# One more wait on GpSimd: the first operation of each attention round starts behind VectorE's FK product

## The chip, the cores and the metric

One NeuronCore of a Trainium2 chip runs the whole program in one launch. The metric is the device time of that core in microseconds, from the launch to the end of the program. A profiled execution has also a span, from its first to its last instruction, which is some two microseconds shorter than its device time.

## The reference

The inputs are float32. Three stages follow each other; only the first is touched by the change.

```python
# stage 1: linear attention with a decaying state, B=4, H=8, S=768, D=48
for t in range(S):
    cur = einsum('bhd,bhe->bhde', u * k[t], v[t])
    y[t] = einsum('bhd,bhde->bhe', r[t], state + cur)
    state = w * state + einsum('bhd,bhe->bhde', k[t], v[t])
# stage 2: x = y as [3072, 384]; tokens with x @ w_skip > 0 go to the expert
#          (of 8) with the largest gate logit: x + gate * (relu(x @ w1[e]) @ w2[e])
# stage 3: ((x @ w1) * (x @ w2)) @ w3 @ w_out
```

## The kernel before

**Stage 1** is worked in 24 tiles of 128 rows. A tile n is a chunk c = n // 2 of 64 time steps of one pair of batches bp = n % 2, all 8 heads side by side. The decay inside a chunk is put into two tables made once (UT, and KU for the key side), so that a tile needs these steps:

- `prep(n)`, VectorE, L360: FK = TB * UT, 128x1024, both operands in SBUF. TB holds r and k of the tile, transposed, and comes by DMA.
- `scores(n)`, TensorE, L367: 16 small matrix products of the two halves of FK into the PSUM bank sc, of which there is one.
- `evac(n)`, VectorE, L372: Fs = sc * mask, one operand in PSUM. It frees sc.
- `prep_k(n)`, GpSimd, L379: kd = k * KU, 128x384, both operands in SBUF; needed by `ds_mm(n)`, which adds the tile to the state on TensorE (L436). The last two tiles need no kd.
- `prep_m(n)`, GpSimd, L385 and L386: m = r * u, then m = k * m, 128x384 each, in SBUF.
- `bonus(n)`, VectorE, L390: z = sum of m over the head's 48 elements.
- `state_copy(n)`: in every second chunk VectorE rescales the state in PSUM (S, L408), and ScalarE copies it to SBUF.
- `y_mm(n)`, TensorE, L420 and L423; `prep_v(n)`, ScalarE, L400; `x_out(n)`, VectorE, L441: xg = y + zv, and two stores of xg from the queue of SyncE.

Beside them every round has fillers. `w_step` prepares the weights of stage 3 on VectorE (their 64-bit words are cut to float32 by the three operations of L112, L115 and L119, the first with one tensor operand and the other two with two operands in SBUF). `keep` puts products of these weights, or empty ones, between the others on TensorE (L712, L256), a fixed number for each round. The routing of earlier tiles (`route_a` to `route_d`, `place`; L471 to L567) is made of small VectorE operations that come in some rounds alone.

The order on each engine is that in which the program writes the calls, since scheduling is manual. The loop over rounds n = 0 to 21 writes, in this order: the load of TB for tile n + 4, `prep(n + 2)`, `state_copy(n + 1)`, `scores(n + 1)`, `prep_k(n + 1)`, `prep_m(n + 2)`, `evac(n + 1)`, `bonus(n + 1)` (in round 21 also `bonus(23)`), in rounds 0 to 2 some constants on GpSimd, one `w_step`, `y_mm(n)`, fillers, routing, the second `w_step` where there is one, `x_out(n)`, `ds_mm(n)`, the load of KV for tile n + 4, `place`, the third `w_step`, routing. A round is named by its n, so round n has FK of tile n + 2, kd of tile n + 1 and m of tile n + 2. FK has three buffers, kd and m have two each.

A GpSimd operation of this loop waits for its data (KV by DMA) and for its buffer (kd for `ds_mm` two tiles back, m for `bonus` two tiles back), and for nothing else. So GpSimd may be ahead of VectorE's place in the round or behind it.

Of the kernel before, what the change touches and what calls it, by code (L numbers as in the profile page):

```python
# [13 lines left out]
ALU = mybir.AluOpType  # L14
# [10 lines left out]
NT = NTOK // P  # L25
# [32 lines left out]
def fused_kernel(ctx, tc, att, kv, wt, u, wg, we, w3, wo, w12, r, k, v, wu, out):  # L58
    nc = tc.nc
# [134 lines left out]
    def load_expert(e, q):  # L194
        raw = stg[(4 * e + q) % 3 // 2].tile([P, 2, 2 * D], F32, name="raw")
        nc.sync.dma_start(out=raw, in_=we[e, :, 2 * q:2 * q + 2, :])
        return raw
# [29 lines left out]
    with tc.manual_schedule():  # L227
# [5 lines left out]
        KV = [[ac.tile([P, 3, NH, HD], F32, name=f"KV{bp}_{j}") for j in range(2)] for bp in range(2)]  # L233
        Ss = [ac.tile([P, NH, HD], F32, name=f"Ss{bp}") for bp in range(2)]
        TB = [ac.tile([P, 2, NH, CH], F32, name=f"TB{j}") for j in range(3)]
        un = ac.tile([P, NH, HD], F32, name="un")

        def load_t(n):
            nc.sync.dma_start(out=TB[n % 3].rearrange("p a h t -> p (a h t)"), in_=att[n])
# [30 lines left out]
        for q in range(2):  # L270
            m = mask[64 * q:64 * q + 64]
# [12 lines left out]
        UT = ac.tile([P, 2, 2, NH, CH], F32, name="UT")  # L284
# [6 lines left out]
        for i in range(6):  # L291
            wn = pw[:, i - 1] if i else wc
            n = 1 << i
# [13 lines left out]
        KU = ac.tile([P, 2, NH, HD], F32, name="KU")  # L307
# [48 lines left out]
        def prep(n):  # L356

            t = TB[n % 3]
            FK = FK_[n] = wk.tile([P, 2, NH, CH], F32, name="FK", bufs=3)
            nc.vector.tensor_tensor(out=FK, in0=t, in1=UT[:, n // 2 % 2], op=ALU.mult)  # L360

        def scores(n):
            FK = FK_[n]
            sc = ps_1.tile([P, 512], F32, tag="sc", name="sc").rearrange("p (h t) -> p h t", h=NH)
            for h in range(NH):
                for m, d in zip(half, dims):
                    nc.tensor.matmul(sc[m, h], FK[d, 1, h], FK[d, 0, h], start=True, stop=True)  # L367
            return sc

        def evac(n, sc):  # L370
            Fs = Fs_[n] = wk.tile([P, NH, CH], F32, name="Fs")
            nc.vector.tensor_tensor(out=Fs, in0=sc, in1=mask[:, None, :].to_broadcast([P, NH, CH]), op=ALU.mult)  # L372

        def prep_k(n):

            c, bp = divmod(n, 2)
            if c < NC - 1:
                kd = kd_[n] = wk.tile([P, NH, HD], F32, name="kd")
                nc.gpsimd.tensor_tensor(out=kd, in0=KV[bp][c % 2][:, 1], in1=KU[:, c % 2], op=ALU.mult)  # L379

        def prep_m(n):

            c, bp = divmod(n, 2)
            m = P_[n] = wk.tile([P, NH, HD], F32, name="m")
            nc.gpsimd.tensor_tensor(out=m, in0=KV[bp][c % 2][:, 0], in1=un, op=ALU.mult)  # L385
            nc.gpsimd.tensor_tensor(out=m, in0=KV[bp][c % 2][:, 1], in1=m, op=ALU.mult)  # L386

        def bonus(n):
            z = z_[n] = wk.tile([P, 32], F32, name="z")[:, 0:NH]
            nc.vector.tensor_reduce(out=z, in_=P_.pop(n), axis=AX.X, op=ALU.add)  # L390

        def prep_v(n, eng=None):
            c, bp = divmod(n, 2)
            v, z = KV[bp][c % 2][:, 2], z_.pop(n)
            zv = zv_[n] = wk.tile([P, NH, HD], F32, name="zv")
            if eng:
                eng.tensor_tensor(out=zv, in0=v, in1=z[:, :, None].to_broadcast([P, NH, HD]), op=ALU.mult)
            else:
                for h in range(NH):
                    nc.scalar.activation(out=zv[:, h], in_=v[:, h], func=AF.Copy, scale=z[:, h:h + 1])  # L400

        def state_copy(n):
            c, bp = divmod(n, 2)
            s = S[bp]
            if c == 0:
                return
            if c % 2 == 0:
                nc.vector.tensor_tensor(out=s, in0=s, in1=w128[:, :, None].to_broadcast([P, NH, HD]),  # L408
                                        op=ALU.mult)
            nc.scalar.copy(out=Ss[bp], in_=s)  # L410

        def y_mm(n, tag="y"):

            c, bp = divmod(n, 2)
            v, Fs, FK = KV[bp][c % 2][:, 2], Fs_.pop(n), FK_.pop(n)
            y = G if n % 2 and n < NT - 2 else ps_1.tile([P, 512], F32, tag=tag, name="y")
            yv = y[:, 0:D].rearrange("p (h d) -> p h d", h=NH)
            for h in range(NH):
                for m in half:
                    nc.tensor.matmul(yv[m, h], Fs[m, h], v[m, h], start=(h == 0), stop=True, skip_group_check=True)  # L420
            for h in range(NH if c else 0):
                for m, d in zip(half, dims):
                    nc.tensor.matmul(yv[m, h], FK[d, 0, h], Ss[bp][d, h], start=False, stop=True,  # L423
                                     skip_group_check=True)
            y_[n] = y
            if n < NT - 2:
                yb[0] = y
# [10 lines left out]
        def x_out(n):  # L438
            c, bp = divmod(n, 2)
            xg = x_[n] = wk.tile([P, D], F32, name="xg", bufs=2)  # L440
            nc.vector.tensor_tensor(out=xg, in0=y_.pop(n)[:, 0:D], in1=zv_.pop(n).rearrange("p h d -> p (h d)"),  # L441
                                    op=ALU.add)
            for q in range(2):
                r0 = (2 * bp + q) * NS + c * CH
                nc.sync.dma_start(out=xm[r0:r0 + CH, :], in_=xg[64 * q:64 * q + 64, :])

        def x_trans(n, bank=None):
            xg = x_.pop(n)
            xb_[n] = T if bank is None else bank
            pT = xb_[n][:, 0:D].rearrange("p (k t) -> p k t", k=ND)  # L450
            for k in range(ND):
                nc.tensor.transpose(pT[:, k], xg[:, P * k:P * k + P], ident)
            xT_[n] = wk.tile([P, ND, P], F32, name="xT", bufs=2)
            nc.scalar.copy(out=xT_[n], in_=pT)
# [219 lines left out]
        def w_step(k):  # L674
            for _ in range(k):
                next(wprep, None)
# [3 lines left out]
        def w_evac(k):  # L680

            while k < len(w_out):
                f, ps = w_out[k]
                nc.scalar.copy(out=W_hi[:, f], in_=ps)
                w_out[k:k + 1] = []
                w_lo.append((f, ps))
# [8 lines left out]
        def w_ready():  # L695
            done.update(fresh[0])
            fresh[:] = fresh[1:] + [[]]
# [29 lines left out]
        def keep(k):  # L727

            due[0] += k
            while due[0] > 0:  # L730
                if next(wmm, None):
                    due[0] -= 4
                else:
                    idle_mm()
                    due[0] -= 2


        prep(0)
        table_k(0)
        load_t(3)  # L740
# [23 lines left out]
        def run_todo(late=False):  # L764
            now, todo[:] = sorted(todo, key=lambda x: x[0] is not logits), []
            for fn, args in now:
                if late and fn is route_b:
                    todo.append((fn, args))
                    continue
                fn(*args)  # L770
                if fn is logits_out:
                    if args[0] in last_of:
                        todo.append((route_a, (last_of[args[0]],)))
                elif fn in NEXT:
                    todo.append((NEXT[fn], args))

        for n in range(NT - 2):
            w_ready()
            if n == NT - 3:
                raws = {q: load_expert(0, q) for q in range(2)}  # L780
            if n + 4 < NT:
                load_t(n + 4)
            prep(n + 2)
            state_copy(n + 1)
            sc = scores(n + 1)
            prep_k(n + 1)
            prep_m(n + 2)
            evac(n + 1, sc)
            bonus(n + 1)
            if n == NT - 3:  # L790
                bonus(NT - 1)
            next(more_consts, None)
            w_step(WN[n][0])
            w_ready()
            y_mm(n)
            keep(4 * WK[n][0])
            run_todo()
            if n > 0:
                x_trans(n - 1)
            prep_v(n + 1)  # L800
            keep(4 * WK[n][1])
            w_step(WN[n][1])
            w_evac(0)
            x_out(n)
            ds_mm(n)
            place_mm(n % 2)
            if n + 4 < NT:
                load_v(n + 4)
            if n < NT - 3:
                place(3)  # L810
            w_step(WN[n][2])
            run_todo(n < NT - 3)
            if n > 0:
                todo.append((logits, (n - 1,)))
            w_evac2()
# [100 lines left out]
    with tc.manual_schedule():  # L916
# [126 lines left out]
        first = {}  # L1043
# [324 lines left out]
```

## Time and profile before

| | us |
|---|---|
| median of 3 runs | 648.27 |
| lowest and highest of them | 647.77, 656.43 |
| the profiled execution, device time | 645.56 |
| its span | 643.8 |
| TensorE busy in the span | 620.2 (96%) |
| VectorE busy | 366.2 (57%) |
| GpSimd busy | 142.8 (22%) |

The loop of stage 1 fills some 14 to 160 us of the span; what follows is the routing's end, the experts to some 330 us and stage 3. Start times in the rows are us from the start of the span. An instruction's duration in the trace runs on while it waits for access inside the engine, so the same operation can show two durations; the idle time in brackets ahead of an operation is what the engine spent with nothing to run, and the name behind the arrow is what ended it.

### The profile page before, as it was taken

The numbers are of one execution on the slowest core, as the hardware profiler recorded it, in microseconds if no ns is written. First come the engines' busy times: TensorE is split into PE (matmuls) and PEld (weight loads), VectorE is DVE, ScalarE is ACT, GpSimd is POOL, SyncE is SP. The second block draws the span as 40 slices with busy tenths as digits, with TensorE's granted clock in tenths as the row PEclk, the third lists the DMA queues.
The fourth block names the chain that finished last, engine by engine and source line by source line (L and its number), as shares of the span: only waits on it lengthen the run. The fifth ranks groups of instructions, "written<-read, shape, count | busy, mean of one in ns | idle before, by whom it ended". The sixth has DMA issues, their size and how long they took to land.

```text
span 643.8 us, 14006 instructions
## 1 busy us (share of the span) xinstructions
PE 620.2 (96%) x5866; PEld 535.6 (83%) x5866; DVE 366.2 (57%) x641; ACT 254.2 (39%) x592; POOL 142.8 (22%) x134
## 2 busy tenths in 40 slices
PE   7989999899989999999999999999999999999996
PEld 6878877788769999999988888888888888888884
DVE  6699999999478789998863312322321321330320
ACT  2555644444346666666542322222322221331220
POOL 4885555554040322333220000000000000000000
PEclk9899999999989999999999999999999999999999
DMA  8889978557158877778211002002002002000001
GB/s 306 347 276 350 342 248 320 175 168 233 48 171 270 294 246 277 273 256 308 92 62 56 0 34 66 1 34 65 1 17 81 2 16 82 0 17 34 0 2 53
DMA packets 26791, 90.53 MB, mean 141 GB/s; under 512 B 4009, under 2 KB 10298, under 8 KB 25696
## 3 DMA queue, kind: packets, MB, share of 16 engines
q1 hardware_dynamic: 24672, 84.11, 37.6%
q0 software_dynamic: 2048, 5.44, 2.5%
q8 instruction: 48, 0.79, 0.5%
q14 instruction: 23, 0.19, 0.1%
HBM read 77.81 MB, written 12.58 MB: 140 GB/s over the span
## 4 chain that ended last, share of the span: by engine, by line
PE 75%; DVE 13%; issue 5%; DMA 4%; POOL 1%; ACT 1%; SPq 1%; DVEq 0%; ACTq 0%; POOLq 0%
PE ab L1131 31%; PE po L1151 15%; PE hp L931 9%; PE y L950 9%; PE wp L712 3%; DMA TB<-in_att 3%; DVE FK L360 3%; PE sc L367 1%; DVE Fs L372 1%; DMA KV<-in_kv 1%; DVE w L119 1%; PE pT L1111 1%; DVE z L390 1%; DVE w L112 1%; DVE w L115 1%
## 5 line engine op out<-in xcount | busy, mean ns | idle before, releaser
L1138 DVE TENSOR_TENSOR p_sb<-ab,a_sb 128x512 f32<-128x512 f32 x48 | 33.2, 691 | 155.6 <-PE ab L1131 155.6
L1131 PE MATMUL ab<-bxh,w12h 128*128 128x512 f32 x288 | 112.3, 390 | 0.6 <-ACT bxh L1170 0.6
L1131 PE MATMUL ab<-bxh,w12l 128*128 128x512 f32 x288 | 112.0, 389 | 0.0
L1131 PE MATMUL ab<-bxl,w12h 128*128 128x512 f32 x288 | 112.0, 389 | 0.0
L1139 ACT CAST ph<-p_sb 128x512 fp32r<-128x512 f32 x48 | 29.8, 621 | 105.9 <-DVE p_sb L1138 105.9
L86 DVE TENSOR_TENSOR elo<-raw,ehi 128x768 fp32r<-128x768 f32 x64 | 60.8, 954 | 8.7 <-ACT ehi L85 8.4
L1131 PEld LDWEIGHTS ab<-bxh,w12h 128*128 128x128 f32 x288 | 54.0, 188 | 12.7 <-ACT bxh L1170 1.5
L1131 PEld LDWEIGHTS ab<-bxl,w12h 128*128 128x128 f32 x288 | 54.1, 188 | 11.6 <-DVE bxl L1172 0.4
L1131 PEld LDWEIGHTS ab<-bxh,w12l 128*128 128x128 f32 x288 | 54.1, 188 | 11.1
L1151 PE MATMUL po<-ph,W_hi 128*128 128x512 f32 x144 | 57.0, 396 | 0.0
L1151 PE MATMUL po<-pl,W_hi 128*128 128x512 f32 x144 | 56.1, 390 | 0.0
L1151 PE MATMUL po<-ph,W_lo 128*128 128x512 f32 x144 | 56.0, 389 | 0.0
L931 PE MATMUL hp<-xh,ehi 128*128 128x256 f32 x192 | 54.5, 286 | 1.3 <-ACT xh L881 1.1
L931 PE MATMUL hp<-xl,ehi 128*128 128x256 f32 x192 | 54.1, 284 | 0.0
L931 PE MATMUL hp<-xh,elo 128*128 128x256 f32 x192 | 54.0, 283 | 0.0
L85 ACT CAST ehi<-raw 128x768 fp32r<-128x768 f32 x64 | 52.6, 828 | 2.8 <-DMA raw<-in_we 2.8
L1140 DVE TENSOR_TENSOR pl<-p_sb,ph 128x512 fp32r<-128x512 f32 x48 | 33.2, 692 | 32.9 <-ACT ph L1139 32.9
L400 ACT ACTIVATE zv<-KV,z 128x48 f32<-128x48 f32 x184 | 44.0, 324 | 16.8 <-DVE z L390 14.9
L712 PE MATMUL wp<-wo_s,w 128*128 128x384 f32 x128 | 50.4, 505 | 0.0
L934 ACT ACTIVATE hh<-hp 128x256 fp32r<-128x256 f32 x64 | 24.6, 385 | 49.5 <-PE hp L931 49.3
L950 PE MATMUL y<-ehi,hh 128*128 128x384 f32 x128 | 43.5, 339 | 0.0
L950 PE MATMUL y<-ehi,hl 128*128 128x384 f32 x128 | 43.2, 337 | 0.0
(207 smaller groups left out, 1174.8 us busy)
## 6 DMA issues: line engine op xcount, KB each, us to landing
raw<-in_we SPq DMA_DIRECT2D x32, 768.0 KB, 4.8
KV<-in_kv SPq DMA_DIRECT2D x24, 576.0 KB, 5.5
TB<-in_att SPq DMA_DIRECT2D x24, 512.0 KB, 7.3
raww<-in_w SPq DMA_DIRECT2D x8, 1024.0 KB, 7.8
raw<-in_w SPq DMA_DIRECT2D x8, 768.0 KB, 6.7
xm<-xg SPq DMA_DIRECT2D x48, 96.0 KB, 3.2
out<-ob SPq DMA_DIRECT2D x18, 256.0 KB, 2.0
x<-xm SPq DMA_DIRECT2D x20, 192.0 KB, 3.0
```

The source lines that it names most:

```text
L85: nc.scalar.copy(out=hi, in_=raw)
L86: (eng or nc.vector).tensor_tensor(out=lo, in0=raw, in1=hi.bitcast(F32), op=ALU.subtract)
L400: nc.scalar.activation(out=zv[:, h], in_=v[:, h], func=AF.Copy, scale=z[:, h:h + 1])
L712: nc.tensor.matmul(ps, w3[:, g], wo_s[:, g], start=(g == 0), stop=(g == NF - 1))
L931: nc.tensor.matmul(hp, a, b, start=(i == 0), stop=(i == 8))
L934: nc.scalar.activation(out=hh, in_=hp, func=AF.Relu)
L950: nc.tensor.matmul(ys[e, t], a[:, P * t:P * t + P], b[:, D:2 * D], start=(f == 0 and i == 0), stop=(f == NF - 1 and i == 2))
L1131: nc.tensor.matmul(q, a, b, start=(i == 0), stop=(i == 8))
L1138: nc.vector.tensor_tensor(out=p_sb, in0=ps[1], in1=a_sb, op=ALU.mult)
L1139: nc.scalar.copy(out=ph, in_=p_sb)
L1140: nc.vector.tensor_tensor(out=pl, in0=p_sb, in1=ph.bitcast(F32), op=ALU.subtract)
L1151: nc.tensor.matmul(po, a[:, f, c], b, start=(i == 0), stop=(i == 3 * NF - 1))
```

## The change

The first GpSimd operation of round n gets one more wait, for the end of FK of the same round. In rounds 0 to 20 this is kd of tile n + 1, and in round 21, which has no kd, the first half of m of tile 23. `prep`, `prep_k` and `prep_m` return their first instruction for it, and `behind` adds a semaphore dependency. No operation is added, removed or put in another place of its engine's order; the calls ahead of the loop (tiles 0 and 1) have no such wait.

```diff
             t = TB[n % 3]
             FK = FK_[n] = wk.tile([P, 2, NH, CH], F32, name="FK", bufs=3)
-            nc.vector.tensor_tensor(out=FK, in0=t, in1=UT[:, n // 2 % 2], op=ALU.mult)
+            return nc.vector.tensor_tensor(out=FK, in0=t, in1=UT[:, n // 2 % 2], op=ALU.mult)
+
+        def behind(later, earlier):
+
+            tc.add_manual_dep(later.ins, earlier.ins.name, mybir.DependencyInfo(
+                mybir.DependencyClass.Sync, mybir.DependencyReason.DATA), reason="two operands from SBUF each")
...
-                nc.gpsimd.tensor_tensor(out=kd, in0=KV[bp][c % 2][:, 1], in1=KU[:, c % 2], op=ALU.mult)
+                return nc.gpsimd.tensor_tensor(out=kd, in0=KV[bp][c % 2][:, 1], in1=KU[:, c % 2], op=ALU.mult)
...
-            nc.gpsimd.tensor_tensor(out=m, in0=KV[bp][c % 2][:, 0], in1=un, op=ALU.mult)
+            first = nc.gpsimd.tensor_tensor(out=m, in0=KV[bp][c % 2][:, 0], in1=un, op=ALU.mult)
             nc.gpsimd.tensor_tensor(out=m, in0=KV[bp][c % 2][:, 1], in1=m, op=ALU.mult)
+            return first
...
-            prep(n + 2)
+            fk = prep(n + 2)
             state_copy(n + 1)
             sc = scores(n + 1)
-            prep_k(n + 1)
-            prep_m(n + 2)
+            behind(prep_k(n + 1) or prep_m(n + 2), fk)
+            if n < NT - 3:
+                prep_m(n + 2)
             evac(n + 1, sc)
             bonus(n + 1)
```

## Rows read from the trace of the kernel before

**Rows 1.** Windows: length; busy (count) of PE, PEld, DVE, ACT, POOL; TensorE clock; DMA share.
```profile
26.00:60.00 34.00, 30.09 (x715) 26.51 (x715) 33.83 (x38) 17.46 (x58) 24.17 (x23) 1.00 0.83 294
60.00:110.00 50.00, 47.72 (x1016) 39.79 (x1016) 49.55 (x75) 26.24 (x87) 30.49 (x23) 1.00 0.87 304
110.00:158.00 48.00, 45.93 (x991) 37.99 (x992) 47.10 (x91) 22.34 (x85) 26.30 (x21) 1.00 0.59 190
```

**Rows 2.** Waits in 26 to 158 us: total, times, longest.
```profile
POOL kd L379 <- PE S L436: 30.0, 13, 3.9
...
PE sc L367 <- DVE Fs L372: 7.7, 7, 2.4
```

**Rows 3.** Timeline, VectorE and GpSimd around FK of round 4.
```profile
36.56 1.98 POOL L379 TENSOR_TENSOR kd<-KV,KU 128x384 f32<-128x384 f32 x1
...
38.07 1.55 DVE L119 SCALAR_TENSOR_TENSOR w<-raww,w 128x1024 int32<-128x1024 int32 x1
...
38.50 1.97 POOL L385 TENSOR_TENSOR m<-KV,un 128x384 f32<-128x384 f32 x1
...
39.55 2.01 DVE L360 TENSOR_TENSOR FK<-TB,UT 128x1024 f32<-128x1024 f32 x1
...
40.55 1.86 POOL L386 TENSOR_TENSOR m<-KV,m 128x384 f32<-128x384 f32 x1
...
42.37 1.00 POOL L379 TENSOR_TENSOR kd<-KV,KU 128x384 f32<-128x384 f32 x1
```

**Rows 4.** Timeline, VectorE and GpSimd at the start of round 10.
```profile
81.89 1.21 DVE L360 TENSOR_TENSOR FK<-TB,UT 128x1024 f32<-128x1024 f32 x1
...
83.02 0.67 DVE L372 TENSOR_TENSOR Fs<-sc,mask 128x512 f32<-128x512 f32 x1
83.62 0.53 DVE L390 TENSOR_REDUCE z<-m 128x8 f32<-128x384 f32 x1
...
84.08 0.67 DVE L112 TENSOR_SCALAR w<-w 128x1024 int32<-128x1024 int32 x1
84.23 1.38 POOL L385 TENSOR_TENSOR m<-KV,un 128x384 f32<-128x384 f32 x1 [0.28 <-DVE z L390]
```

**Rows 5.** VectorE's groups by line, 25.5 to 158 us: busy, mean ns, idle before.
```profile
L360 DVE TENSOR_TENSOR FK<-TB,UT 128x1024 f32<-128x1024 f32 x20 | 30.3, 1517 | 4.2 <-DMA TB<-in_att 4.2
L372 DVE TENSOR_TENSOR Fs<-sc,mask 128x512 f32<-128x512 f32 x20 | 13.5, 676 | 0.0
L119 DVE SCALAR_TENSOR_TENSOR w<-raww,w 128x1024 int32<-128x1024 int32 x8 | 11.8, 1480 | 0.0
L115 DVE SCALAR_TENSOR_TENSOR w<-raww,w 128x1024 int32<-128x1024 int32 x8 | 11.5, 1436 | 0.0
...
L112 DVE TENSOR_SCALAR w<-w 128x1024 int32<-128x1024 int32 x8 | 6.7, 833 | 0.0
...
L552 DVE TENSOR_TENSOR val<-r_sg,val 128x6 bf16<-128x6 f32 (+1 forms) x3 | 2.0, 654 | 0.1
...
L471 DVE TENSOR_TENSOR r_oh<-io_f,r_mi 128x48 f32<-128x48 f32 (+1 forms) x3 | 1.1, 373 | 0.1
```

**Rows 6.** VectorE by source line, L115: durations least/median/most, first and last start.
```profile
L115 DVE SCALAR_TENSOR_TENSOR w<-raww,w x8: 1206/1212/1968, 35.8 to 131.3; 128x1024 int32<-128x1024 int32 x8
```

**Rows 7.** Timeline, TensorE, the last places where it waits for VectorE.
```profile
98.58 1.15 PE L367 MATMUL sc<-FK 48*64 48x64 f32 x32 [0.60 <-DVE Fs L372]
...
124.97 0.92 PE L436 MATMUL S<-KV,kd 64*48 64x48 f32 x32
127.96 1.15 PE L367 MATMUL sc<-FK 48*64 48x64 f32 x32 [2.07 <-DVE Fs L372]
```

**Rows 8.** Timeline, VectorE in round 21.
```profile
156.37 1.21 DVE L360 TENSOR_TENSOR FK<-TB,UT 128x1024 f32<-128x1024 f32 x1
...
158.11 0.99 DVE L390 TENSOR_REDUCE z<-m 128x8 f32<-128x384 f32 x2
160.16 0.56 DVE L441 TENSOR_TENSOR xg<-G,zv 128x384 f32<-128x384 f32 x1 [1.06 <-PE G L465]
```

## The prediction

> **What bounds the kernel now.** I read the windows first, since the change lives in one stage alone. In each of the three stretches from 26 to 158 us [rows 1] the reader is to see two engines that are nearly full: VectorE works 33.83 of 34, 49.55 of 50 and 47.10 of 48 us, and TensorE 30.09, 47.72 and 45.93. TensorE's idle time is what is left: 3.9 + 2.3 + 2.1 = 8.3 us. The waits come next [rows 2]: nearly all of that, 7.7 us in 7 places, is TensorE's scores waiting for VectorE's Fs, which frees the PSUM bank. So VectorE's pace sets the loop, and TensorE is close behind it: **no saving on VectorE can give more than some 8.3 us**, about 1.3% of the run. The last place where TensorE waits is 127.96 us [rows 7]; from there it runs without a gap to the end of the loop. The end therefore moves with VectorE's progress up to that point. GpSimd's largest wait, 30.0 us for its kd buffer, costs nothing: it is early.
>
> Then the timeline. Around FK of round 4 [rows 3] GpSimd and VectorE take turns. The weight operation L119 runs from 38.07, m asks at 38.50 and takes 1.97 us; FK asks at 39.55, when L119 lets go, and takes 2.01; the next m asks at 40.55 and takes 1.86. Alone, FK takes 1.21 [rows 4] and a GpSimd product 1.00 [rows 3]. So a GpSimd product and a VectorE operation with two operands in SBUF don't overlap: who asks later stands still, and FK lost 2.01 - 1.21 = 0.80 us. Fs, with one operand in PSUM, is never stretched (mean 676 ns in 20, 0.67 alone) [rows 4, 5].
>
> What this costs before: for each VectorE instruction of rounds 2 to 20 I took its duration less the shortest of its form. The groups of [rows 5] hold it: FK 20 x (1.517 - 1.204) = 6.3 us; the wide weight operations 8 x (1.480 - 1.206) + 8 x (1.436 - 1.206) + 8 x (0.833 - 0.67) = 5.3 us (the clean L115 in [rows 6], L112 in [rows 4]); the rest, routing products above all (seven groups of three, means from 654 down to 373 ns, some 200 ns clean) and the narrower weight operations, about 7.8. Together **19.4 us in 19 rounds**.
>
> **The change, step by step.** It adds 22 waits and no work. Behind the waiting kd stand both m operations of its round (in rounds 0 to 2 constants too); who needs them is `ds_mm` and `bonus` of the next round. From FK's start, kd would ask at 1.29 us (FK's 1.21 and 0.08: z of [rows 4] ends at 84.15 and the m that waits for it starts at 84.23) and the last m would end by about 4.5 even with two stops. The z that reads it comes after the next round's FK and Fs, 1.74 us into that round; a round lasts 6.6 us on average (20 FKs [rows 5] in 132 us), so z comes at some 8.3 us against 4.5. Nobody waits: this part costs nothing as long as a round is longer than 4.5 - 1.74 = 2.8 us. Round 21 is the exception, since its z of tile 23 stands in the same round. m would ask at 1.29 and its second half end by some 3.4 us after FK's start, while z now starts at 1.74 + 0.46 = 2.2 [rows 8]: 1.2 us later. Behind it xg waited for TensorE for 1.06 us anyway [rows 8], so about 0.2 us is left. SyncE's loads of KV wait for a kd of the round before, which stays earlier than they are; DMA is 0.59 to 0.87 busy [rows 1].
>
> What is moved is where GpSimd's three products stand beside VectorE. Clean starts from FK's start [rows 4]: Fs 1.13, z 1.73, the first weight operation 2.19, each 0.47 later in the ten rounds with the state's rescale. I take 0.82 us as the time for which a product shuts VectorE out (FK's 0.80, rounded up by its entry), the one that asks first goes first, and go through the rounds.
> - kd runs from 1.29 to about 2.2, beside Fs and z, which it can't stop. FK is free of it: the 0.8 us of [rows 3] is gone.
> - The first m asks at about 2.27. Without rescale the weight operation asked at 2.19 and goes first; m enters as it ends. With rescale m is first, and the operation, due at 2.66, waits until about 3.1: 0.4 us.
> - The second m meets what comes then: 0.66 us where a second weight operation follows directly (rounds 2 to 6), otherwise it begins beside xg, which covers 0.47 of its 0.82, and 0.3 us falls on the operation behind.
>
> Rounds 2 to 6, three weight operations each, give 3 x 0.97 + 1.06, and 1.90 in round 3, where round 2's constants on GpSimd still push the product of before into FK: 5.9 us (6.6 now). Rounds 7, 10 to 13, 16 and 17, one operation ahead of xg, give 0.7 with rescale and 0.3 without: 3.8 us (3.4 now). The seven rounds with much routing (8, 9, 14, 15, 18 to 20) give 6.6 us (9.4 now), the least certain part, as products of 0.2 us either meet an m or don't. Sum 16.2 against 19.4: **3.2 us less on VectorE**. Up to round 15, which is what counts for the wait at 127.96, it is 13.3 against 17.1: 3.85 us earlier. TensorE could take that: its own work is done at 124.97 + 0.92 = 125.89, and with the earlier wait at 98.58 moved by 2.1 us it is free at 123.8, ahead of 127.96 - 3.85 = 124.1 [rows 7].
>
> Unknown is the hold. At 0.87 us instead of 0.82 some forty meetings, two a round, cost 0.05 each, 2 us, and 1.85 is left. I take the middle, -2.85, and round 21's +0.2: **-2.6 us** (rounded). The profiled execution, 645.56 us for a span of 643.8, would come to about 643. The median of the runs is 2.7 above that execution, and I forecast against the median: 648.27 - 2.6 = **645.7**. Ends of this term: -8.3 (all of TensorE's idle time) and +3 (below).
>
> By the Trainium skill (SBUF — State Buffer, Who interferes with whom) issue order decides which of the two blocks and the later one blocks fully; this trace agrees, FK's 2.01 us behind an m, and on that rule alone the change picks another loser and frees nobody.
>
> **The rivals.**
> - *The collisions only move.* Each FK freed is a weight or routing operation stopped. For it: of the three kinds above one gets worse, and the gain is mostly in the routing rounds. Against it: kd's 19 products get cover that they often lack now. Time: 19.4 us stay, 648.3.
> - *Slower: m wins the race to the first weight operation.* Without rescale that operation is ahead by only 2.27 - 2.19 = 0.08 us. If GpSimd wakes faster or its kd is shorter by that much, m enters first, the operation stands 0.8 us, and the second m still finds the next one. In the nine rounds without rescale from 2 to 20 that is 9 x 0.7 = 6.3 us more: 16.2 + 6.3 = 22.5 against 19.4, 3.1 slower, 651.4. It decides at about 2.19 us after FK's start.
> - *All of TensorE's slack.* If kd's share of the meetings, a third, simply vanishes, 6.5 us go; with better luck in routing it ends at the 8.3: 640 to 642.
> - *The wait does nothing.* That needs kd to be behind FK already. In [rows 3] it isn't: round 4's kd starts at 36.56, its FK at 39.55. So it is in nearly every round, since kd's buffer is free early; this is nearly excluded: 648.3.
>
> **How the numbers follow.** Forecast, 643 to 647.5: 0.55. Collisions only move: 0.20. Slower: 0.14. All of the slack: 0.08. Nothing: 0.03. 2%, about what a measurement of this kernel can tell from no change, is 13 us; no case reaches it, as the gain is bounded by 8.3 and the worst loss, both m's stopping VectorE for a full 0.82 in each of 19 rounds, would be 31.2 - 19.4 = 11.8. So 0.95 within, 0.02 faster, 0.03 slower. Range: from 641, into the last gain, to 652, beyond the slower rival; three executions of the same kernel lie between 645.6 and 648.3, which both ends take in.
>
> **What would show it.** Right: FK at 1.21 us in nearly all rounds (mean 1517 ns now), kd at 1.00 in all and starting 0.08 us after FK; the stretch moved to L112, L115 and L119; TensorE's wait before scores of round 16 ending near 124 us, and the stages behind shifted whole. Wrong: FK's time kept, or VectorE's sum of stretch at 19 or more; z waiting for m in a round other than 21; FK waiting for TB, which would say that DMA takes the place of the meetings; or an end that doesn't follow TensorE's last wait.

## The result and the profile after

| | before | after |
|---|---|---|
| median of 22 runs each, us | 652.80 | 645.19 |
| lowest and highest | 645.51, 656.43 | 641.11, 648.45 |
| ratio after / before, 95% interval | | 0.9906 [0.9877, 0.9934] |
| profiled execution, device time | 645.56 | 643.80 |

The changed kernel is 0.9% faster, some 6 us, within the 2% that were given for no clear change. Every ratio here is one of mean times, without executions more than 1.5% above the fastest of their kernel; the medians of the table lie further apart, 7.6 us. Run once more beside other kernels on one chip (after_again) it came to 0.9932 [0.9898, 0.9967], 4.4 us. The forecast was a gain of 2.6 us: the sign is right, the size is about half of what was measured.

The windows of the changed kernel, in the order of columns of [rows 1], the last number being the GB/s that the DMA engines moved (the line numbers of its kernel are 5 to 7 higher than before):

```profile
26.00:60.00 34.00, 31.00 (x655) 27.23 (x652) 33.48 (x40) 17.09 (x58) 19.86 (x22) 0.85 0.85 312
60.00:110.00 50.00, 50.00 (x1057) 41.82 (x1053) 49.02 (x78) 26.10 (x87) 29.18 (x24) 1.00 0.87 311
110.00:158.00 48.00, 47.78 (x1019) 39.80 (x1018) 43.49 (x89) 22.33 (x85) 22.95 (x21) 1.00 0.60 193
```

From 60 us on TensorE is full in this execution (50.00 of 50, 47.78 of 48), and VectorE has room in the last stretch, 43.49 of 48 where it had 47.10. But the first stretch has something that before had not, a mean granted clock of 0.85, and a TensorE that ran slowly there is behind afterwards. The profile of after_again, the same kernel with a clock of 1.00 in all three stretches, reads:

```profile
26.00:60.00 34.00, 32.71 (x756) 28.71 (x754) 33.83 (x40) 17.72 (x60) 20.68 (x22) 1.00 0.86 301
60.00:110.00 50.00, 48.98 (x1055) 40.76 (x1052) 49.48 (x78) 26.04 (x87) 29.39 (x24) 1.00 0.87 316
110.00:158.00 48.00, 46.15 (x973) 38.56 (x968) 44.16 (x90) 22.58 (x86) 22.92 (x21) 1.00 0.61 199
```

```profile
125.10 1.15 PE L372 MATMUL sc<-FK 48*64 48x64 f32 x32 [1.85 <-DVE Fs L377]
```

There VectorE is still the fuller engine up to 110 us, and TensorE's idle time has fallen from 8.3 to 4.2 us; its last wait for VectorE, 1.85 us, ends at 125.10. So at full clock the bound has not changed hands before round 16: VectorE and TensorE have come close to each other.

Waits of the first profile in 26 to 158 us, total, times, longest:

```profile
POOL kd L384 <- DVE FK L360: 55.1, 18, 5.0
...
PE sc L372 <- DVE Fs L377: 2.5, 3, 1.5
...
DVE z L396 <- POOL m L391: 0.7, 1, 0.7
```

GpSimd now stands 55.1 us in front of kd, for FK, and nobody minds: TensorE's wait for Fs fell from 7.7 us in 7 places [rows 2] to 2.5 in 3 (3.8 in 3 in after_again), and the one wait of VectorE for m is the one of round 21. The start of round 10, VectorE and GpSimd in order of time:

```profile
80.24 1.21 DVE L360 TENSOR_TENSOR FK<-TB,UT 128x1024 f32<-128x1024 f32 x1
...
81.60 1.00 POOL L384 TENSOR_TENSOR kd<-KV,KU 128x384 f32<-128x384 f32 x1 [4.89 <-DVE FK L360]
...
82.44 0.71 DVE L112 TENSOR_SCALAR w<-w 128x1024 int32<-128x1024 int32 x1
82.56 1.45 POOL L390 TENSOR_TENSOR m<-KV,un 128x384 f32<-128x384 f32 x1
```

Beside [rows 4] this is the replay of the prediction: kd takes 1.00 us under Fs and z, the weight operation asks at 2.20 us after FK's start and is 0.12 us ahead of m (0.08 was forecast), m waits for it and takes 1.45. VectorE's groups, as in [rows 5] (25 to 155 us, the same instructions):

```profile
L360 DVE TENSOR_TENSOR FK<-TB,UT 128x1024 f32<-128x1024 f32 x20 | 25.1, 1255 | 3.7 <-DMA TB<-in_att 3.7
...
L115 DVE SCALAR_TENSOR_TENSOR w<-raww,w 128x1024 int32<-128x1024 int32 x8 | 11.8, 1479 | 0.0
L119 DVE SCALAR_TENSOR_TENSOR w<-raww,w 128x1024 int32<-128x1024 int32 x8 | 11.6, 1450 | 0.0
L112 DVE TENSOR_SCALAR w<-w 128x1024 int32<-128x1024 int32 x8 | 7.2, 901 | 0.0
...
L573 DVE TENSOR_TENSOR s_v<-r_o,val 128x240 bf16<-128x240 bf16 x5 | 3.6, 716 | 0.0
```

FK's mean fell from 1517 to 1255 ns, 5.2 us in 20. Two of the three weight operations got a little worse (L112 from 833 to 901, L115 from 1436 to 1479; L119 went from 1480 to 1450). And s_v, of which the prediction took no notice, fell from this row of the kernel before:

```profile
L567 DVE TENSOR_TENSOR s_v<-r_o,val 128x240 bf16<-128x240 bf16 x5 | 6.0, 1198 | 0.0
```

One FK is still stretched, in round 14, where the last m of a short round 13 runs into it, and a new wait of VectorE, 1.06 us for ScalarE, stands at the end of that round (at 113.36 in after_again, as long):

```profile
104.62 2.02 DVE L360 TENSOR_TENSOR FK<-TB,UT 128x1024 f32<-128x1024 f32 x1
...
113.71 0.56 DVE L698 TENSOR_TENSOR W_lo<-wp,W_hi 128x384 fp32r<-128x384 f32 x1 [1.06 <-ACT W_hi L690]
```

### The profile page after: what moved, and what is told of

The parts are those of the page before. It is cut to its first block, busy times and chain, and to the rows that moved or that the text cites. A ratio compares the mean times of both kernels' runs of the same rounds, so it can differ in the third digit from the quotient of the medians.

```text
span 642.1 us, 14003 instructions
## 1 busy us (share of the span) xinstructions
PE 623.2 (97%) x5866; PEld 538.4 (84%) x5866; DVE 361.7 (56%) x641; ACT 253.9 (40%) x592; POOL 130.1 (20%) x134
## 4 chain that ended last, share of the span: by engine, by line
PE 74%; DMA 9%; DVE 8%; issue 5%; ACT 1%; POOL 1%; SPq 0%; POOLq 0%; ACTq 0%; DVEq 0%
PE ab L1138 31%; PE po L1158 15%; PE wp L718 5%; PE hp L938 5%; PE y L957 4%; DMA xr<-xm,sidx 3%; DMA xm<-yo,sidx 3%; PE sc L372 2%; PE S L442 2%; DMA TB<-in_att 2%; PE G L429 1%; PE G L426 1%; PE y L426 1%; DMA xm<-xg 1%; PE y L429 1%
## 5 line engine op out<-in xcount | busy, mean ns | idle before, releaser
L718 PE MATMUL wp<-wo_s,w 128*128 128x384 f32 x128 | 51.9, 517 | 0.0
```

Of the source, the lines that this page charges most:

```text
L718: nc.tensor.matmul(ps, w3[:, g], wo_s[:, g], start=(g == 0), stop=(g == NF - 1))
```

## The experiments

Each of the twelve stood beside the kernel before on one chip, with 6 or 12 executions. The last column counts executions whose mean granted clock over the span was 0.988 or more, a cut chosen after seeing the runs, which is used under before_fill and after_fill; beside these twelve the kernel before had 13 of 87 (the clocks of its first 22 are not on record), the changed kernel, its first runs and after_again together, 17 of 34. The cut doesn't tell where in the span the clock was low: the first profile of the changed kernel, with a low stretch in the loop, has 0.988, and that of after_again, without one behind 26 us there, 0.989.

| run | ratio, 95% interval | median, us | clock 0.988 or more |
|---|---|---|---|
| after_again | 0.9932 [0.9898, 0.9967] | 643.62 | 7 of 12 |
| wait_z | 1.0049 [1.0012, 1.0086] | 654.01 | 0 of 12 |
| wait_prev | 0.9998 [0.9959, 1.0036] | 650.52 | 2 of 12 |
| early_only | 0.9972 [0.9936, 1.0008] | 650.08 | 2 of 12 |
| late_only | 0.9960 [0.9929, 0.9992] | 647.86 | 2 of 12 |
| early16 | 0.9935 [0.9909, 0.9962] | 645.82 | 6 of 12 |
| late17 | 0.9982 [0.9945, 1.0018] | 649.62 | 2 of 12 |
| m_memset | 0.9874 [0.9824, 0.9925] | 642.72 | 4 of 6 |
| before_fill | 0.9983 [0.9946, 1.0019] | 647.41 | 9 of 12 |
| after_fill | 0.9879 [0.9832, 0.9926] | 642.64 | 5 of 6 |
| best_a | 0.9893 [0.9836, 0.9951] | 641.96 | 5 of 6 |
| best_b | 0.9890 [0.9856, 0.9924] | 642.57 | 9 of 12 |

"Stretch" below is summed as in the prediction (duration less the shortest of the same form, rounds 2 to 20), but with the shortest taken over all these profiles, which also shows forms that were stretched each time before: 26.3 us before, 20.7 and 21.7 in the two profiles of the changed kernel.

**after_again**: no edit.

> The changed kernel once more, beside the others on one chip. Expected: 0.985 to 0.994 of the kernel before, FK at 1.21 us in all rounds but one, the stretch of VectorE's operations in rounds 2 to 20 near 17.7 us (23.4 before, with 0.40 us as the clean time of s_v).

The ratio and FK came as expected, with one exception, in round 14. The stretch fell by 4.6 us, from 26.3 to 21.7, where 5.7 were expected (23.4 to 17.7, on another base of shortest durations).

**wait_z**: is it the place of kd, or only that FK is left alone?

```diff
-            nc.vector.tensor_reduce(out=z, in_=P_.pop(n), axis=AX.X, op=ALU.add)
+            return nc.vector.tensor_reduce(out=z, in_=P_.pop(n), axis=AX.X, op=ALU.add)
...
-            behind(prep_k(n + 1) or prep_m(n + 2), fk)
+            if n == NT - 3:
+                behind(prep_m(n + 2), fk)
+            evac(n + 1, sc)
+            z = bonus(n + 1)
             if n < NT - 3:
+                behind(prep_k(n + 1), z)
                 prep_m(n + 2)
-            evac(n + 1, sc)
-            bonus(n + 1)
```

Round 21 keeps its wait for FK, and the order on each engine is as it was.

> kd waits for the end of z of the same round in place of the end of FK; no work is left out. Theory (a GpSimd product and a VectorE operation with two SBUF operands exclude each other, and the change gains because kd then stands beside Fs and z): kd now meets the first weight operation and pushes both m operations by about 1 us, so the last m falls into the next FK; the stretch in rounds 2 to 20 rises to about 31 us, some 7 above before and 13 above the change, and the run is 5 to 8 us slower than before (ratio 1.008 to 1.013). Rival (what counts is only that nothing of GpSimd's queue is ahead of the round, so that FK starts unhindered): as fast as the change, 0.990, with FK at 1.21 us.

Slower than before, as the theory has it and the rival has not, though by 3.2 us where 5 to 8 were expected; the stretch rose to 33.6 us (31 expected, on the narrower base). In round 4 kd starts after z, in place of FK, and each of the three products meets one of VectorE's:

```profile
42.74 1.18 POOL L384 TENSOR_TENSOR kd<-KV,KU 128x384 f32<-128x384 f32 x1 [2.75 <-DVE z L396]
43.09 1.64 DVE L115 SCALAR_TENSOR_TENSOR wo_s<-raww,wo_s 128x768 int32<-128x768 int32 x1
43.88 1.71 POOL L390 TENSOR_TENSOR m<-KV,un 128x384 f32<-128x384 f32 x1
...
45.12 1.28 DVE L119 SCALAR_TENSOR_TENSOR wo_s<-raww,wo_s 128x768 int32<-128x768 int32 x1
45.67 1.60 POOL L391 TENSOR_TENSOR m<-KV,m 128x384 f32<-128x384 f32 x1
46.33 2.02 DVE L360 TENSOR_TENSOR FK<-TB,UT 128x1024 f32<-128x1024 f32 x1
```

kd starts 1.2 us after FK's end, 1.7 with the rescale, where the change has 0.14; that is enough to put the last m into the next FK, whose 2.02 us are those of [rows 3]. So the wait gains by where it puts the products, and 1.1 to 1.5 us decide its sign.

**wait_prev**: as many waits, pointing to a place that kd reaches later anyway.

```diff
-        prep(1)
+        fk_before = prep(1)
...
-            behind(prep_k(n + 1) or prep_m(n + 2), fk)
+            behind(prep_k(n + 1) or prep_m(n + 2), fk_before)
+            fk_before = fk
```

> The same number of added waits, but kd waits for FK of the round before in place of that of its own round. Theory: in nearly all rounds kd starts later than that anyway, so it is where it was, FK is stretched as before (6.3 us in 20) and the time is that of the kernel before, 0.998 to 1.002. Rival (a wait at kd by itself, wherever it points, brings the gain, by holding GpSimd back or by its semaphore): 0.990 to 0.995.

0.9998 [0.9959, 1.0036], as the theory has it: a wait as such does nothing that can be told from none.

**early_only and late_only**: which rounds count?

```diff
-            behind(prep_k(n + 1) or prep_m(n + 2), fk)
+            first = prep_k(n + 1) or prep_m(n + 2)
+            if n <= 15:          # late_only: n > 15
+                behind(first, fk)
```

> The wait in rounds 0 to 15 alone. Theory (VectorE's gain counts up to TensorE's last wait for it, in round 16): the whole gain but 1 us at most, 0.989 to 0.993. Rival (each round gives its share of the gain): 16 of 22 rounds, 0.993 to 0.994 at the change's 0.990.

> The wait in rounds 16 to 21 alone. Theory (TensorE has no wait left behind round 16 and sets the end): no gain, 0.999 to 1.002, although VectorE's stretch in rounds 16 to 20 falls by some 2 us. Rival (each round gives its share): 6 of 22 rounds, 0.997.

Both went against the theory as I had put it: the first 16 waits gave less than expected and the last six gave something. The profile of early_only shows the mistake, VectorE at the end of round 15:

```profile
120.48 0.99 DVE L477 TENSOR_TENSOR r_q<-r_pr,r_ohb 128x48 f32<-128x48 f32 x1
...
121.74 0.77 DVE L481 TENSOR_SCALAR r_hf<-r_rk 128x6 f32<-128x6 f32 x1
...
122.87 0.95 DVE L477 TENSOR_TENSOR r_o<-r_ohb,r_o 128x48 bf16<-128x48 bf16 x1
```

Elsewhere in this profile r_q, r_hf and r_o take some 0.2 us each at their shortest. Here kd of rounds 16 and 17 and m of tile 18, which nothing holds any more, have run ahead of VectorE into round 15 (kd starts at 118.47 and 122.76, m at 119.43 and 121.49) and stretch them by some 2 us. So the wait of round n also spares the operations at the end of round n - 1, and a cut behind round 15 gives part of round 15 away; TensorE then waited 4.33 us, up to 127.00.

**early16 and late17** move the cut by one round.

```diff
-            if n <= 15:
+            if n <= 16:          # late17: n > 16
```

> The wait in rounds 0 to 16, one more than in early_only. Theory (the wait of round n spares the operations at the end of round n - 1, which the kd that ran ahead would have stopped; TensorE has no wait left behind round 16): round 15 loses the three stretches of early_only (0.79, 0.60 and 0.75 us) and the whole gain of the change is there, 0.990 to 0.994 of the kernel before, within 1 us of the change. Rival (each round's wait gives the same share): 17 of 22, 0.993 to 0.995, and no jump against early_only.

> The wait in rounds 17 to 21 alone. Theory: no gain, 0.998 to 1.002, while late_only with round 16 gave 0.996. Rival (each round's wait gives the same share): 5 of 22, 0.998, hard to tell from the theory by time; the profile tells whether FK of tile 18 starts where it did before.

early16 has the changed kernel's ratio, late17 none that can be told from 1. From FK of round 2 to FK of round 16 it takes 97.1 us in early16 and in after_again, 99.6 in early_only and 99.8 before; so that one wait is worth 2.5 us there. By time alone the intervals of early_only and early16 overlap; the starts in the profiles decide. What counts are the waits up to round 16.

**m_memset**: take the stretch away.

```diff
-            first = nc.gpsimd.tensor_tensor(out=m, in0=KV[bp][c % 2][:, 0], in1=un, op=ALU.mult)
-            nc.gpsimd.tensor_tensor(out=m, in0=KV[bp][c % 2][:, 1], in1=m, op=ALU.mult)
+            first = nc.gpsimd.memset(m, 0.0)
+            nc.gpsimd.memset(m, 0.0)
```

> The changed kernel in which GpSimd's two m products of each tile are replaced by two fills of m with zero: they write as many elements and read nothing. The u term of the attention is left out by that. Theory (a VectorE operation with two SBUF operands stands still only against a GpSimd operation that reads SBUF, and TensorE is the next bound): VectorE's stretch in rounds 2 to 20 falls from about 17.7 us to under 3, TensorE waits for Fs hardly at all, and the time falls by no more than 3 us against the change, 0.983 to 0.991 of the kernel before. Rival 1 (VectorE is still the bound behind the change): 8 us or more below the change, under 0.980. Rival 2 (any GpSimd operation stops VectorE): the stretch stays above 8 us.

VectorE's and, last, GpSimd's groups (25 to 153 us):

```profile
L360 DVE TENSOR_TENSOR FK<-TB,UT 128x1024 f32<-128x1024 f32 x19 | 23.1, 1218 | 6.1 <-DMA TB<-in_att 6.1
...
L115 DVE SCALAR_TENSOR_TENSOR w<-raww,w 128x1024 int32<-128x1024 int32 x8 | 9.7, 1218 | 0.0
...
L112 DVE TENSOR_SCALAR w<-w 128x1024 int32<-128x1024 int32 x8 | 5.9, 737 | 0.0
...
L573 DVE TENSOR_TENSOR s_v<-r_o,val 128x240 bf16<-128x240 bf16 x4 | 1.6, 396 | 0.0
```

```profile
L391 POOL MEMSET m<- 128x384 f32 x19 | 10.2, 536 | 1.1
```

FK and s_v have no fill beside them here, but the wide weight operations have, and the fill runs inside them:

```profile
88.93 1.21 DVE L119 SCALAR_TENSOR_TENSOR w<-raww,w 128x1024 int32<-128x1024 int32 x1
89.03 0.42 POOL L391 MEMSET m<- 128x384 f32 x1
...
124.92 0.68 DVE L112 TENSOR_SCALAR w<-w 128x1024 int32<-128x1024 int32 x1
125.03 0.93 POOL L391 MEMSET m<- 128x384 f32 x1
```

The stretch fell to 3.3 us (under 3 were expected), some 18 less than in the changed kernel, with GpSimd still writing m twice a round (what the kernel leaves out is the u term). A fill doesn't stop a VectorE operation with two operands in SBUF, and isn't stopped by it; a product, which reads, does and is. And the time hardly followed: 642.7 us; among executions with a clock of 0.988 or more the median is 642.45 of four, against 642.61 of seventeen for the changed kernel. Eighteen microseconds less on VectorE bought no time that can be told with these counts, and rival 1 falls. In this profile TensorE waits for Fs once behind 26 us, 0.45 us, and is full from 110 on; but its own clock is low twice in the loop (28 to 39 and 55 to 59 us), so that it isn't shown what this kernel takes at full clock. Its lowest time, 638.99, is 2.1 us below the changed kernel's 641.11.

**before_fill and after_fill**: what else is in the gain? In the changed kernel's first profile TensorE's rows around the wait of round 4 read:

```profile
41.06 1.15 PE L372 MATMUL sc<-FK 48*64 48x64 f32 x32 [1.50 <-DVE Fs L377]
...
43.18 1.92 PE L429 MATMUL G<-Ss,FK 48*64 48x48 f32 x32
...
53.75 1.10 PE L429 MATMUL y<-Ss,FK 48*64 48x48 f32 x32
```

```profile
42.00:54.00 12.00, 12.00 (x191) 10.23 (x187) 11.58 (x14) 7.43 (x24) 6.32 (x7) 0.57 0.90 341
```

After a wait of 1.50 us the same 32 products take 1.92 us instead of 1.10, and the granted clock is 0.57 in these 12 us, mostly at 1.2 GHz. Behind 26 us in the loop such a stretch, of 10 to 14 us, stands in the profiles of late17 (from 42 us, at a wait of 2.20), late_only (78, 1.85), wait_z (86, 2.48), early_only (125, in a wait of 4.33) and m_memset (28, behind waits of 0.90 and 0.45) too, and in none of before, after_again and early16. (Shorter ones, of 3 to 8 us, stand ahead of 26 us in most profiles, before and after_again among them.) Each came with a wait of TensorE, but not each wait brought one: before had 2.07 us at 127.96 [rows 7], after_again 1.85 at 125.10 and early16 1.83 at 124.56, at full clock behind them. It is not in the program alone but in the execution, since the changed kernel has profiles with and without it; that more waits of TensorE give it more chances is a guess. The fills give TensorE empty products in the three rounds of its long waits:

```diff
+            for _ in range({4: 15, 10: 7, 16: 18}.get(n, 0)):
+                nc.tensor.matmul(T[:, D:512], zb[:, 0:P], zb[:, 0:P], start=True, stop=True, skip_group_check=True)
             sc = scores(n + 1)
```

> The kernel before with 15, 7 and 18 small empty products on TensorE ahead of the scores of rounds 4, 10 and 16, the places where its profile shows TensorE waiting for 2.41, 1.19 and 2.07 us. They need nothing and stand in time that was idle; nothing is left out. Theory (some 2 us of the change's gain come from the granted clock: a wait of TensorE is followed in some executions by 10 to 14 us at 1.2 GHz in the middle of the loop): fewer such stretches, a median 2 to 3 us below the kernel before (0.995 to 0.997) and a narrower spread. Rival (the clock falls for reasons that have nothing to do with these waits): 1.000 or 1 us slower, with the same spread.

> The changed kernel with the same empty products. Theory: hardly any execution in the upper group (646 to 648 us) is left, the median near 643 us, 3 us below before_fill, which is the change's gain without the clock. Rival: as the change, two groups, or 1 to 2 us slower where the products outlast the shorter waits.

before_fill can't be told from the kernel before by its ratio. But 9 of its 12 executions have a clock of 0.988 or more, where the kernel before had 13 of 87, and its profile has no low-clock stretch behind 26 us in the loop. after_fill has 5 of 6, though its own profile does have one, from 37 us, where the empty products themselves had waited 1.90 us for ScalarE:

```profile
35.32 1.00 PE L792 MATMUL T<-zb 128*128 128x128 bf16 x15 [1.90 <-ACT xT L460]
```

At 0.988 or more, after_fill's median of 642.52 lies 4.1 us below before_fill's 646.64: with TensorE kept busy the wait of the change is worth what it is worth without. That the fill keeps the clock up is clear from the counts of before_fill (5 of 6 against 17 of 34 say little by themselves); what it does to the mean time is not.

**best_a and best_b**: the changed kernel with the fills of rounds 10 and 16, without the wait in round 21; best_b also has two more units of filler products of TensorE in round 3.

```diff
+            for _ in range({10: 7, 16: 18}.get(n, 0)):
+                nc.tensor.matmul(T[:, D:512], zb[:, 0:P], zb[:, 0:P], start=True, stop=True, skip_group_check=True)
             sc = scores(n + 1)
-            behind(prep_k(n + 1) or prep_m(n + 2), fk)
+            first = prep_k(n + 1) or prep_m(n + 2)
+            if n < NT - 3:
+                behind(first, fk)
```

```diff
-WK = [(1, 1)] * 9 + [(1, 2)] * 13
+WK = [(1, 1)] * 3 + [(1, 3)] + [(1, 1)] * 5 + [(1, 2)] * 13
```

> The changed kernel without the wait of round 21 (z of tile 23 waited 0.7 to 0.8 us for its m there), with empty products of TensorE ahead of the scores of rounds 10 and 16 alone (7 and 18), as those of round 4 waited 1.9 us for ScalarE in after_fill. Theory: the wait of TensorE in round 16 no longer ends in a stretch at 1.2 GHz; 0.988 to 0.992, at most 2 us below the change. Rival: as the change.

> best_a with two more units of filler in round 3 (empty products that wait for nothing), in the 1.2 to 1.5 us that TensorE waits ahead of the scores of round 4. Theory: the stretch at 1.2 GHz that begins at 36 to 44 us is gone as well, most executions at 641 to 644 us, 0.985 to 0.990. Rival: the fillers only delay TensorE: 0.990 to 0.994, two groups as with the change.

Both beat the kernel before by 1.1%, as expected, with the lowest medians of all, 641.96 and 642.57; but best_b still has two groups, 7 executions up to 642.72 and 5 from 645.84, as its rival has it, and their intervals overlap the changed kernel's, so neither is shown to be better than it. Taking the wait out of round 21 exchanged one thing for another. In place of z, VectorE's FK of tile 23 now stands, and xg waits for TensorE either way:

```profile
151.44 2.01 DVE L360 TENSOR_TENSOR FK<-TB,UT 128x1024 f32<-128x1024 f32 x1
...
156.10 0.56 DVE L447 TENSOR_TENSOR xg<-G,zv 128x384 f32<-128x384 f32 x1 [1.14 <-PE G L471]
```

## Why the prediction was right, and where its size was off

**The bound** held. VectorE set the loop with TensorE close behind, and in after_again it still does up to round 16, with TensorE's idle time halved. The ceiling of 8.3 us wasn't passed: m_memset, with hardly a stretch left on VectorE, gained 1.3%, some 8 us, of which the clock is a part (646.50 to 642.45, 4 us, among executions at 0.988 or more).

**FK goes free and kd hides under Fs and z**: right in every round but one. kd takes 1.00 us (mean 1002 ns in 19), the weight operation stays ahead of m in the rounds without rescale, by 0.12 us where 0.08 was reckoned. kd started 0.14 us behind FK's end, not 0.08, which is what widened the margin. wait_prev shows that the wait does nothing without its place, wait_z that 1.1 to 1.5 us later the sign turns.

**The replay of the stretch** up to round 15 forecast 3.85 us less. Measured, over the same rounds and with the wider choice of shortest durations, it is 19.8 us before and 16.0 and 16.2 in the two profiles of the changed kernel: 3.6 to 3.8 less. So the hold of 0.82 us was right (FK and s_v each lost 0.80), and the 0.87 for which the prediction took 1 us off again was not needed. Over rounds 2 to 20 it forecast 3.2 less and found 5.6 and 4.6 (26.3 to 20.7 and 21.7). One term was mis-sized: s_v had been stretched in all five of its instances, so the shortest of them, 1.20 us, was taken as its clean time, and it is 0.40. It held 4.0 us of stretch that the prediction didn't see, and the change freed three of the five in one profile and two in the other, 2.4 and 1.6 us. It lies in the routing rounds, which the prediction had called its least certain part.

**From VectorE to the end.** Between two executions without a low-clock stretch behind 26 us in the loop, the profiles of before and of after_again, the step that was forecast can be read by itself. FK of tile 18 starts at 125.62 before and 122.76 after, stage 3's first product at 336.26 and 333.36, and the device time is 645.56 and 642.76: **2.8 us, where -2.85 and, with round 21, -2.6 had been forecast**; the stages behind shifted whole. TensorE's wait before scores of round 16 ended at 125.10 (124.1 forecast). The rows of before and of after_again:

```profile
125.62 1.22 DVE L360 TENSOR_TENSOR FK<-TB,UT 128x1024 f32<-128x1024 f32 x1
...
336.26 0.50 PE L1131 MATMUL ab<-bxh,w12h 128*128 128x512 f32 x1 [0.56 <-ACT bxh L1170]
```

```profile
122.76 1.22 DVE L360 TENSOR_TENSOR FK<-TB,UT 128x1024 f32<-128x1024 f32 x1
...
333.36 0.50 PE L1138 MATMUL ab<-bxh,w12h 128*128 128x512 f32 x1 [0.56 <-ACT bxh L1177]
```

That the two numbers meet is luck. From FK of tile 4 to FK of tile 18 VectorE is busy 3.8 us less (98.83 to 95.03), but only 2.7 us were saved there (99.80 to 97.06): the other 1.06 are the new wait of VectorE's W_lo for ScalarE's W_hi in round 14, which stands in both profiles of the changed kernel and not in that of before, and which the prediction had put at nothing. An allowance of 1 us for a longer hold, which didn't come, paid for it. Nor is 2.8 us shown to be the gain at equal clock, since it is one execution of each: the lowest times on record, 645.41 and 641.11, lie 4.3 apart.

**Round 21**: z waited 0.68 and 0.83 us for m, of the 1.2 forecast; xg behind it waited 0.88 and 0.72 us for TensorE all the same, so the cost was about nothing.

**The size against the median** is the step that fell short: 4.4 to 6.1 us were measured, not 2.6. The prediction set the gain of one profiled execution against the median, and took 645.56 and three runs as typical; that execution was nearly the lowest of the kernel, whose median over 22 runs is 652.80. That the median after, 645.19, is within 0.6 us of the forecast 645.7 is luck too: the base was 4.5 us too low, and the gain 5 us smaller than the 7.6 between the medians. The range had the same weak footing: it was held against three executions between 645.6 and 648.3, while the fourth then on record, 656.43, lay outside it. The granted clock was no term of its sum. Split at the cut of 0.988, the kernel before has medians of 646.50 (13 executions) and 650.69 (74), the changed one 642.61 (17) and 647.08 (17): 3.9 and 3.6 us less within each group. The rest would come from the larger share with a higher clock, 0.50 against 0.15, times the 4.2 us between the groups: some 1.5, together a little over 5. That fits, and the reason would be that fewer waits of TensorE leave fewer places for a low-clock stretch. The counts of before_fill speak for it; but the cut was chosen afterwards, before_fill's ratio doesn't show the gain in time, the cut doesn't separate the executions by stretches in the loop, and so this last part is argued, not shown.

**The rivals.** That collisions only move is true of L112 and L115, which got worse, and false of the sum. m won the race to the weight operation in no round without rescale of after_again, and in one of the first profile, round 6, where Fs came late in the low-clock stretch. All of TensorE's slack was not reached: 2.5 and 3.8 us of waits for Fs are left. That the wait does nothing is excluded by wait_prev. The rule that issue order decides who blocks (the Trainium skill, SBUF — State Buffer, Who interferes with whom) agrees with the rows of [rows 3] and of wait_z, but it doesn't follow that someone must lose: kd now runs its 1.00 us beside Fs and z, which aren't stretched.

## What to carry to other kernels

When two engines shut each other out, hold one's operation until the other does something that doesn't need the shared access; a wait is worth only the place that it points to, and here 1.1 to 1.5 us decided between gain and loss. The shortest duration of an operation is its clean time only if some instance ran alone; where all meet the same neighbour, as s_v did, look for it in a run without that neighbour. And where the granted clock differs between executions of one program, compare several of them before taking a profiled one as typical.

## What the runs showed of the hardware

- A small operation with two operands in SBUF stands as long as a large one: s_v, 240 elements per partition, took 1.20 us beside GpSimd's product and 0.40 with nothing of GpSimd's beside it (m_memset), the same 0.80 that FK lost.
- VectorE's operations with one tensor operand were stopped too: L112 took up to 1.33 us in the changed kernel at 0.68 alone, r_hf 0.77 in early_only at 0.17. In m_memset, where GpSimd only writes m, the weight operations with two operands are clean with a fill inside them (1.21 us at 88.93, the fill 0.42), while a fill that asked during L112 took 0.93 us in place of 0.42 (125.03). This agrees with the Trainium skill (SBUF — State Buffer, Who interferes with whom): two operands in SBUF contend with GpSimd's reads alone, while a tensor_scalar can contend with its writes too.
- TensorE ran at 1.2 GHz for 10 to 14 us in the middle of a full loop in some executions and not in others of the same program. In six profiles this came with a wait of 1.5 to 4.3 us, in m_memset with waits of 0.90 and 0.45; waits of 1.8 to 2.4 us in before, after_again and early16 had no such effect.
